# Group 0 of a Fourier-mixing network on one Trainium2 core: the mixture laid into y's tile before y arrives, and the second weight ahead of group 1

## The chip, the cores and the metric

The kernel runs on one core of a Trainium2 chip. The metric is the device time of one execution in microseconds, as the median of several runs; the runs and the profile of the kernel before are shown below. The engines of the core work side by side, each through its own list of instructions in order: TensorE (matmuls, PE in the trace), VectorE (DVE), ScalarE (ACT), GpSimd (POOL) and SyncE (SP), which here only issues DMAs.

## The reference

For x of 8 batches, 3136 tokens and 256 channels, a filter is applied in the frequency domain along the tokens; then a Fourier mixing over tokens and channels is added, the sum is normalised over its channels and goes through two weight matrices with a ReLU between them.

```python
X = np.fft.rfft(x, axis=1)
y = np.fft.irfft(X * (filt_r + 1j * filt_i)[None], n=3136, axis=1)
mixed = np.real(np.fft.fft(np.fft.fft(y, axis=1), axis=2))
u = y + mixed
un = (u - mean(u)) / sqrt(var(u) + 1e-6)          # over the 256 channels
out = u + np.maximum(un @ w_ch1, 0) @ w_ch2       # 256 -> 1024 -> 256
```

## The kernel before, in words

Fourier transforms are done as matmuls in stages. For batch b, `s1_b_*` and `s2_b_*` are the forward stages, `i1_b_*` and `y_b_*` the inverse ones. The spectrum, folded to half its length, lies in a ring `eo` of 1920 slots; a slot stands for a pair of tokens. Batch 0 is done in float32, ahead of everything; batches 1 to 7 in pairs of float16 numbers (a high half and the low rest). Between the stages data go through DRAM to be laid out anew: `d<-ast`, `at<-d`, `d<-bt`, `b<-d`, `dy<-ys`, `y<-dy`.

The second part of the network works on 49 groups of twice 128 slots. For a group g: `mix_g`, the mixture, is formed from the ring on TensorE (line 904); VectorE adds it to y, scaled, in eight instructions (line 914) and takes moments; ScalarE the root (968), VectorE the scales (974 to 978); `un`, `u` high and low halves (1058, 1061, GpSimd 1062); two DMA transposes give `ut` (1063); eight first products `h_g_f` of six matmuls 128 x 512 (1087), whose ReLU goes in halves through ScalarE (1097) and VectorE (1098); eight second products of twelve matmuls each into `acc_g` (1117); and y + beta acc goes out (1126). Group 0 is a special case (`prepare_first`): its y comes straight from the PSUM banks of the inverse stage, and its u is transposed on TensorE (`flip`, tiles `utt`).

The weights come as 64-bit words. They are widened to float32 (`widen`, four VectorE operations and one of ScalarE for each of eight parts), squared (`wsq`, ScalarE), bounded by a power of two (`bound_weights`, `pow2`, with one matmul `pb_w` that spreads a column) and split into halves (`split_weights`, `lower_weights`); parts 0 to 3 are the first weight, 4 to 7 the second. The tables LOAD_AT, WIDEN_AT, SQUARE_AT, BOUND_AT and SPLIT_AT say at which step each is put into the program (`weigh(n)`).

The program is written as generators (`advance` for the forward stages, `give` for the inverse ones, `prepare` for a group) and a loop over q = 8 g + f, in which the first product of (g, f) and the second product of the one LAG = 2 behind stand in turn. A scheduler orders the instructions of each engine; `after(...)` holds one behind a marked other. `warm(n)` puts n matmuls without use on TensorE (52 after the start, in the tile `idle`), so that it doesn't stand still.

Where instructions are named s2_1_0, i1_1_6 or y_1_0, this is the tile that they write: stage, batch, part.

## Time and profile before

| | us |
|---|---|
| runs | 1442.11, 1444.62, 1441.51 |
| median | 1442.11 |
| the profiled execution, its own time | 1443.13 |
| its span | 1441.4 |

In the profiled execution the engines were busy, in us of the span: TensorE 1399.5 (97%), VectorE 1045.9 (73%), ScalarE 758.2 (53%), GpSimd 508.3 (35%). The mean granted clock of TensorE was 0.996 of 2.4 GHz. The profile is read by its time lines (start of an instruction or of a run of equal ones, its length, and in brackets how long the engine stood idle before it and what ended that), by groups of instructions, and by stretches of time (length, then the busy time and the count of instructions of PE, PE's weight loads, DVE, ACT and POOL, the granted clock as a share of 2.4 GHz, the share of the DMA engines and GB/s). Matmuls are pipelined, so the length of a run of matmuls is longer than the time until the next can start.

### The profile page before, as it was taken

What the parts mean: (1) busy time and instruction counts of PE and PEld (TensorE: products, weight loads), DVE (VectorE), ACT (ScalarE), POOL (GpSimd) and SP (SyncE); (2) the same over time, 40 slices, a digit from 0 to 9 for tenths busy, and PEclk for the clock granted to TensorE, in tenths of its full rate; (3) what the DMA queues carried; (4) which work ended last, traced back from release to release, by engine and by line L of the source; (5) the groups of instructions that cost most, each with busy time, mean ns of one, the idle gap of its engine ahead of it and who ended that gap; (6) DMA issues with size and microseconds to landing.
All of it is one profiled execution on the core that took longest, in us unless ns stands there. A gap on an engine that the chain in (4) does not pass through costs nothing.

```text
span 1441.4 us, 30003 instructions
## 1 busy us (share of the span) xinstructions
PE 1399.5 (97%) x11274; PEld 946.7 (66%) x11274; DVE 1045.9 (73%) x2327; ACT 758.2 (53%) x1422; POOL 508.3 (35%) x641
## 2 busy tenths in 40 slices
...
GB/s 362 209 218 243 228 176 250 205 228 209 264 136 193 243 173 232 173 222 187 195 209 200 224 180 226 144 229 233 132 258 156 230 189 193 110 157 78 86 59 30
DMA packets 434221, 276.42 MB, mean 192 GB/s; under 512 B 218796, under 2 KB 401084, under 8 KB 434076
## 3 DMA queue, kind: packets, MB, share of 16 engines
...
q14 instruction: 57, 0.47, 0.1%
q10 hardware_dynamic: 128, 0.05, 0.0%
HBM read 124.41 MB, written 99.17 MB: 155 GB/s over the span
## 4 chain that ended last, share of the span: by engine, by line
PE 64%; DMA 10%; POOL 6%; issue 5%; DVE 4%; ACT 3%; SPq 2%; DVEq 0%; POOLq 0%; ACTq 0%
PE h L1087 25%; PE acc L1117 24%; PE s L495 3%; DMA at<-d 2%; PE y L814 2%; DMA x<-x 2%; PE mix L904 2%; DMA d<-ast 2%; POOL u L1062 1%; PE s L481 1%; PE i L694 1%; PE s L592 1%; PE i L696 1%; PE i L695 1%; POOL ef L639 1%
## 5 line engine op out<-in xcount | busy, mean ns | idle before, releaser
L1117 PE MATMUL acc<-w2s,h 128*128 128x256 f16 x4704 | 594.2, 273 | 2.0 <-DVE y L1126 1.4
L1087 PE MATMUL h<-ut,home 128*128 128x512 f16 x2352 | 580.2, 380 | 12.8 <-DVE h L1098 8.2
L1117 PEld LDWEIGHTS <-h 128*128 128x128 f16 x4704 | 455.8, 98 | 147.8 <-issue 18.2
L1097 ACT ACTIVATE h<-h 128x512 f16<-128x512 f32 x392 | 233.1, 595 | 383.3 <-PE h L1087 374.4
L1098 DVE SCALAR_TENSOR_TENSOR h<-h,h 128x512 f16<-128x512 f32 x392 | 267.5, 684 | 203.5 <-ACT h L1097 202.7
L1087 PEld LDWEIGHTS <-home 128*128 128x128 f16 x2352 | 221.5, 98 | 221.5 <-issue 31.7
L1062 POOL TENSOR_TENSOR u<-un,u 128x512 f16<-128x512 f32 x96 | 110.8, 1172 | 665.3 <-ACT u L1061 612.3
L914 DVE SCALAR_TENSOR_TENSOR y<-mix,alpha,y 128x508 f32<-128x508 f32 (+1 forms) x360 | 152.6, 475 | 1.7 <-DMA d<-bt 0.6
L1058 ACT ACTIVATE un<-y,sb 128x256 f32<-128x256 f32 x192 | 99.7, 590 | 33.4 <-DVE sb L978 29.6
L609 POOL TENSOR_TENSOR yt<-yt,t 128x224 f32<-128x224 f32 x108 | 73.3, 679 | 121.8 <-DVE t L601 48.8
L698 DVE TENSOR_TENSOR bt<-i,bt 112x512 f16<-112x512 f32 x98 | 66.6, 684 | 43.4 <-ACT bt L697 41.6
L825 ACT ACTIVATE ys<-y,alpha 128x512 f32<-128x512 f32 x98 | 66.5, 686 | 57.8 <-PE y L814 57.6
L1126 DVE SCALAR_TENSOR_TENSOR y<-acc,beta,y 128x512 f32<-128x512 f32 x98 | 71.1, 745 | 25.6 <-PE acc L1117 25.5
L697 ACT CAST bt<-i 112x512 f16<-112x512 f32 x98 | 56.8, 584 | 54.9 <-PE i L696 50.2
L639 POOL TENSOR_TENSOR ef<-yt 128x224 f32<-128x224 f32 x112 | 73.3, 674 | 33.2 <-ACT wsq_w L1148 15.7
L597 DVE SCALAR_TENSOR_TENSOR yt<-s,pF,ft 128x448 f32<-128x448 f32 x98 | 65.8, 674 | 26.3 <-PE s L593 19.3
L623 POOL TENSOR_TENSOR home<-yt,home 128x448 f16<-128x448 f32 x77 | 79.5, 1035 | 13.7 <-ACT home L622 13.6
L610 POOL TENSOR_TENSOR yt<-yt,t 128x224 f32<-128x224 f32 x108 | 74.7, 693 | 0.0
L962 DVE BATCH_NORM_STATS2 st<-y 128x6 f32<-128x256 f32 x196 | 72.8, 410 | 0.2
L306 DVE TENSOR_REDUCE mx<-x 112x1 f32<-112x1024 f32 x42 | 51.0, 1214 | 25.2 <-DMA x<-x 24.8
L601 DVE SCALAR_TENSOR_TENSOR t<-s,pF,ft 128x448 f32<-128x448 f32 x98 | 65.9, 674 | 0.0
L669 POOL TENSOR_TENSOR eo<-ef,eo 128x448 f16<-128x448 f32 (+6 forms) x55 | 51.6, 941 | 35.6 <-ACT eo L668 34.2
...
## 6 DMA issues: line engine op xcount, KB each, us to landing
...
```

What stands on the lines that cost most here:

```text
L609: nc.gpsimd.tensor_tensor(yh[:, 0], yh[:, 0], t2v[:, 1], op=ALU.subtract)
L610: marks["sum"] = nc.gpsimd.tensor_tensor(yh[:, 1], yh[:, 1], t2v[:, 0], op=ALU.add).ins
L623: nc.gpsimd.tensor_tensor(ylo, ytv, yhi, op=ALU.subtract)
L639: nc.gpsimd.tensor_tensor(ef[:, i], yt[:, 0, i], yt[:, 1, i], op=o)
L914: nc.vector.scalar_tensor_tensor(out, p, al, y, op0=ALU.mult, op1=ALU.add)
L962: nc.vector.bn_stats(st[:m, 2 * t + k], y[:m, t, k])
L1058: nc.scalar.activation(un[:m, k], y[:m, t, k], AF.Identity, bias=sb[:m, i, 1:2], scale=sb[:m, i, 3:4])
L1062: marks["u16", g] = nc.gpsimd.tensor_tensor(u16[:m, :, :, 1], unv, u16[:m, :, :, 0], op=ALU.subtract).ins
L1087: marks["pe"] = nc.tensor.matmul(p[:, c0 : c0 + n].rearrange("p (t k q) -> p t k q", k=2, q=m), homes["w1s"][:, d, hw, 128 * f : 128 * f + ...
L1097: marks["relu"] = nc.scalar.activation(h[:, 0, :nt], p[:, :nt], AF.Relu).ins
L1098: marks["h"] = nc.vector.scalar_tensor_tensor(h[:, 1, :nt], p[:, :nt], 0.0, h[:, 0, :nt], op0=ALU.max, op1=ALU.subtract).ins
L1117: nc.tensor.matmul(acc[:m, k], h[:, hh, c0 : c0 + m], w2s[:, f, hw], start=f == 0 and k == 0 and i == 0, stop=f == 7 and k == 1 and i == 2,)
```

## The change

For group 0 the mixture is copied out of PSUM already scaled (`near`, and `point` for the single row at half the sampling frequency), and laid into y's tile by two VectorE additions and a copy and, for the single row, by two GpSimd additions and a ScalarE copy. When y comes, one addition for each of the two tiles is left. Both tiles then have one root and one set of scales. The high halves of u are formed by ScalarE straight from y; `un`, in float32, goes to VectorE and is used for the low halves alone. Of the 52 matmuls without use behind the start 20 are left: 8 ahead of the mixture where there were 18, none behind it where there were 10, and 6 behind each of y_2 and y_3 where there were 4 behind each of y_2 to y_7. y_4 to y_7 stand behind the transposes of u.

In the head the parts of the second weight are widened, squared, bounded and split during the eight first products of group 0, which stand in one run on four PSUM banks; then all 96 second products of group 0, and group 1 (mixture, addition, `prepare`) behind the 28th of them. The filters' bound is taken later, and the first weight's earlier. Parts 4 and 5 of the weights are loaded to other buffers than before (LOAD_IN). The first forward stage of batch 1 comes later in the list of TensorE.

```diff
@@ constants
-LOAD_IN = ("b2", "b2", "ys", "ys", "b2", "b2", "ys", "ys")
-WIDEN_AT = (31, 33, 37, 41, 58.3, 58.3, 74, 74)
-SQUARE_AT = (44, 46, 58.1, 58.1, 68, 68, 1002, 1002)
-BOUND_AT = (58.2, 1003)
+LOAD_IN = ("b2", "b2", "ys", "ys", "ys", "ys", "b2", "b2")
+WIDEN_AT = (31, 33, 37, 41, 57.5, 1002, 1004, 1006)
+SQUARE_AT = (38, 42, 46, 47, 66, 1003, 1005, 1007)
+BOUND_AT = (56, 1008)
...
@@ turning u on TensorE (flip)
-            nc.tensor.transpose(pt[:q, i, :m], src[:, i], ident16[:m, :m])
+            with after("turn"):
+                marks["turn"] = nc.tensor.transpose(pt[:q, i, :m], src[:, i], ident16[:m, :m]).ins
...
@@ inverse step of batch 0
-                if j == 26:
-                    idle.append(ps_o.tile([128, 512], F32, tag="pso", name="idle"))
-                    warm(18, "i1", ("pb", "F"), p=idle[0])
...
-            with after("pe") if c == 0 and b else after("warm" if c < 8 else "pe") if b == 0 else nullcontext():
+            with after("pe") if c == 0 and b else after("warm" if c < 4 else "turn") if b == 0 else nullcontext():
...
-            if b == 0 and c < 8:
-                warm(4, "i2", p=idle[0])
-            with after("utt") if b == 0 else nullcontext():
+            if b == 0 and c < 4:
+                warm(6, "i2", p=idle[0])
+            with after("utt", ("cast", 0)) if b == 0 else nullcontext():
...
@@ group 0
-        nc.scalar.copy(near, pm)
-        marks["near"] = nc.scalar.copy(point[:1, 0], fix[0][2]).ins
-        pm, fix = near, [(t, row, point[:1, 0], a) for t, row, _, a in fix]
+        al = alphas[0]
+        nc.scalar.activation(near, pm, AF.Copy, scale=al[:, 0:1])
+        (t0, row, pn, _), = fix
+        marks["near"] = nc.scalar.activation(point[row, 0], pn, AF.Copy, scale=al[row, 0:1]).ins
+        y = mp.tile([128, 2, 2, 256], F32, tag="y", name="y_0", bufs=4)
+        yh = y.rearrange("p t k (h c) -> p t (k h) c", h=2)
+        even, odd = (
+            near[:, :, c0 : c0 + 127].unsqueeze(2).to_broadcast([128, 2, 2, 127]) for c0 in (1, 129)
+        )
+        nc.vector.tensor_tensor(yh[:, :, 0:4:3, 1:], even, odd, op=ALU.add)
+        nc.vector.tensor_tensor(yh[:, :, 1:3, 1:], even, odd, op=ALU.subtract)
+        nc.vector.tensor_copy(y[..., 0:129:128], near[:, :, 0:129:128].unsqueeze(2).to_broadcast([128, 2, 2, 2]))
+        for h, o in ((1, ALU.add), (0, ALU.subtract)):
+            with after("sum"):
+                marks["sum"] = nc.gpsimd.tensor_tensor(
+                    yh[row, t0, 2 + h, 1:], point[row, 0, 1:128], point[row, 0, 129:], op=o
+                ).ins
+        nc.scalar.copy(y[row, t0, 1, 0:129:128], point[row, 0, 0:129:128])
         yield
-        y = mp.tile([128, 2, 2, 256], F32, tag="y", name="y_0", bufs=4)
         ut = mp.tile([128, 2, 8, 128], F16, tag="ut", name="ut_0", bufs=2)
         mv, st, sb = small(0)
-        al = alphas[0]
         for t in range(2):
-            add(y[:, t], pm[:, t], al, sums[t])
-            for tf, row, pn, _ in fix:
-                if tf == t:
-                    add_nyquist(y[row, t, 1], pn, al[row], sums[t][row, 1])
+            nc.vector.tensor_tensor(y[:, t], sums[t], y[:, t], op=ALU.add)
             moments(0, y, [(t, groups[0][t])], st, mv)
-            roots(0, sb, mv, [(128, slice(2 * t, 2 * t + 2))])
-            yield
+        yield
+        parts = [(128, slice(0, 4))]
+        roots(0, sb, mv, parts)
+        scales(0, sb, mv, parts)
+        yield
         for t in range(2):
-            scales(0, sb, mv, [(128, slice(2 * t, 2 * t + 2))])
-            yield
             un = mp.tile([128, 2, 256], F32, tag="un", name=f"un_0_{t}", bufs=2)
             u16 = mp.tile([128, 2, 2, 2, 128], F16, tag="u16", name=f"u16_0_{t}", bufs=2)
-            unv = un.rearrange("p k (d q) -> p k d q", q=128)
             for k in range(2):
                 i = 2 * t + k
-                if t and k:
-                    nc.vector.tensor_scalar(un[:, k], y[:, t, k], sb[:, i, 3:4], sb[:, i, 1:2], op0=ALU.mult, op1=ALU.add)
-                else:
-                    nc.scalar.activation(un[:, k], y[:, t, k], AF.Identity, bias=sb[:, i, 1:2], scale=sb[:, i, 3:4])
-            marks["cast", 0] = nc.scalar.copy(u16[:, :, :, 0], unv).ins
+                marks["cast", 0] = nc.scalar.activation(
+                    u16[:, k, :, 0],
+                    y[:, t, k].rearrange("p (d q) -> p d q", q=128),
+                    AF.Identity,
+                    bias=sb[:, i, 1:2],
+                    scale=sb[:, i, 3:4],
+                ).ins
+                nc.vector.tensor_scalar(un[:, k], y[:, t, k], sb[:, i, 3:4], sb[:, i, 1:2], op0=ALU.mult, op1=ALU.add)
+            unv = un.rearrange("p k (d q) -> p k d q", q=128)
...
@@ first product
-        p = ps_h.tile([128, 512], F32, tag="psh", name=f"h_{g}_{f}")
+        pool, tag = (ps_o, "pso") if g == 0 and f % 4 > 1 else (ps_h, "psh")
+        p = pool.tile([128, 512], F32, tag=tag, name=f"h_{g}_{f}")
...
@@ the head of the main program
+    idle.append(ps_o.tile([128, 512], F32, tag="pso", name="idle"))
+    warm(8, "i1", ("pb", "F"), ("pb", "w1"), p=idle[0])
     for _ in mixture(0):
         pass
     first_group = prepare_first()
     next(first_group)
+    advance(59)
+    for ch in (2, 3, 6):
+        fold_of[0](ch)
     while come[0] < 1 + WAIT + 2:
-        weigh(63 + come[0])
-        if come[0] == 1:
-            warm(10, "mix", p=idle[0])
+        weigh(60 + come[0])
         give(come[0] + 1)
-    for i, _ in enumerate(first_group):
-        weigh(68 + i)
-        give(min(come[0] + 1, KEPT))
+    next(first_group)
+    give(come[0] + 2)
+    for _ in first_group:
+        pass
...
@@ the loop over groups
+            catch_up(8 if q == 8 else min(q - LAG, 2 * (q - 8) + 1))
         if g < ng:
             first_product(g, f)
-        if q == 0:
+        weigh(1002 + q)
+        if q == 7:
+            for part in range(4):
+                split_weights("w2", part)
             work = prepare(1)
-            for _ in range(AHEAD):
-                next(work, None)
-        if q == 1:
-            weigh(1002)
-        if q == 4:
-            weigh(1003)
-        if q in (4, 5):
-            split_weights("w2", 2 * q - 8)
-            split_weights("w2", 2 * q - 7)
-        for n, part, ch in ((2, 1, 4), (6, 0, 5), (6, 0, 6), (8, 1, 5), (9, 1, 6)):
+        for n, part, ch in ((3, 1, 2), (7, 0, 4), (8, 1, 3), (9, 0, 5), (9, 1, 4), (10, 1, 5), (11, 1, 6)):
             if q == n:
                 fold_of[part](ch)
         if q > 1:
             next(halves, None)
-        if f == 8 - AHEAD:
+        if f == 8 - AHEAD and g or q == 7:
             for _ in work:
                 pass
             if g + 2 < ng:
                 work = prepare(g + 2)
-        next(work, None)
+        if q > 7:
+            next(work, None)
         if q >= 8:
             catch_up(min(q - LAG + 1, 2 * (q - 8) + 2))
         give(min(come[0] + 1, soon(32 * q + SOON)))
-        advance(min(int(STEPS * (1 + min((q + 1) / RISE, (q + 1) / per + EARLY))), STEPS + 3 + 3 * (q - 3 if q > 3 else 0) if q < 16 else NB * STEPS))
-        for ahead in [2] * (q == 3) + [g + 3] * (f == 6):
+        advance(min(int(STEPS * (1 + min((q + 1) / RISE, (q + 1) / per + EARLY))), STEPS + 3 + 4 * (q - 6 if q > 6 else 0) if q < 14 else NB * STEPS))
+        for ahead in [2] * (q == 7) + [3] * (q == 11) + [g + 3] * (f == 6 and g > 0):
```

On VectorE, for group 0 (the tile y_925 is y of group 0, y_0_911 and y_1_918 are the PSUM banks of the inverse stage, st and mv the moments). Before:

```order
L914 SCALAR_TENSOR_TENSOR y_925<-near,alpha_652,y_0_911 128x4x127
L914 SCALAR_TENSOR_TENSOR y_925<-near,alpha_652,y_0_911 128x4
L914 SCALAR_TENSOR_TENSOR y_925<-near,alpha_652,y_925 128x2x127 x2
L914 SCALAR_TENSOR_TENSOR y_925<-near,alpha_652,y_1_918 128x4x127
L914 SCALAR_TENSOR_TENSOR y_925<-near,alpha_652,y_1_918 128x4
L914 SCALAR_TENSOR_TENSOR y_925<-point,alpha_652,y_0_911 1x2x127
L914 SCALAR_TENSOR_TENSOR y_925<-point,alpha_652,y_0_911 1x2
L962 BN_STATS st_928<-y_925 128x6
L914 SCALAR_TENSOR_TENSOR y_925<-near,alpha_652,y_925 128x2x127 x2
L914 SCALAR_TENSOR_TENSOR y_925<-point,alpha_652,y_925 1x127 x2
```

In the changed kernel (y_858 is y of group 0, y_0_907 and y_1_914 the banks; `size` belongs to a weight's widening):

```order
L997 TENSOR_TENSOR y_858<-near 128x2x2x127
L998 TENSOR_TENSOR y_858<-near 128x2x2x127
L999 COPY y_858<-near 128x8
L1156 SCALAR_TENSOR_TENSOR home<-size_882,home 128x512
L1010 TENSOR_TENSOR y_858<-y_0_907,y_858 128x512
L959 BN_STATS st_923<-y_858 128x6 x2
L960 BN_AGGR mv_922<-st_923 128x2 x2
L1010 TENSOR_TENSOR y_858<-y_1_914,y_858 128x512
L959 BN_STATS st_923<-y_858 128x6 x2
L960 BN_AGGR mv_922<-st_923 128x2 x2
L971 RECIPROCAL sb_924<-sb_924 128x4
```

Four scaled additions for each tile and four for the single row behind the banks have become two additions and a copy ahead of them and one addition for each tile behind.

On TensorE, from the first product of group 0 to that of group 1 (h_g_f a first product, acc_g_t the sums of the second ones of tile t, h16_g_f what they take, eo the ring, mix_g the mixture of group g, home the first weight, y_0_10 an inverse stage of batch 0). Before:

```order
L1087 MATMUL h_0_0_1100<-ut_0_926,home_596 128x512
L904 LDWEIGHTS eo_595
L904 MATMUL mix_1_1110<-mix_86,eo_595 128x129
...
L1087 MATMUL h_0_1_1171<-ut_0_926,home_596 128x512
...
L1117 LDWEIGHTS h16_0_6_1346
L1117 MATMUL acc_0_1_1429<-w2s_93,h16_0_6_1346 128x256
L1087 LDWEIGHTS home_596
L1087 MATMUL h_1_0_1442<-ut_1_1135,home_596 128x512
```

In the changed kernel:

```order
L1129 LDWEIGHTS h16_0_2_1073
L1129 MATMUL acc_0_0_1279<-w2s_93,h16_0_2_1073 128x256
L801 MATMUL y_0_10_1133<-b2_0_5_905,i2f_85 112x512
L801 MATMUL y_0_11_1149<-b2_0_5_905,i2f_85 112x512
L901 LDWEIGHTS eo_601
L901 MATMUL mix_1_1205<-mix_86,eo_601 128x129
...
L901 MATMUL mix_1_1205<-mix_86,eo_601 128x127
...
L1129 MATMUL acc_0_1_1280<-w2s_93,h16_0_7_1184 128x256
L901 LDWEIGHTS eo_601
L901 MATMUL mix_2_1394<-mix_86,eo_601 128x129
...
L1099 LDWEIGHTS home_602
L1099 MATMUL h_1_0_1381<-ut_1_1230,home_602 128x512
```

Mixture 1 has moved from behind the first of group 0's first products to a place behind the 28th of its second products, and all second products of group 0, not 84 of 96, stand ahead of h_1_0; mixture 2 begins right ahead of h_1_0.

On GpSimd, in batch 1's second step (yt a part of the filtered spectrum, ef and eo the folding into the ring, the rows with home and y_3 the low halves of z, the input of stage i1; u_4 the low halves of group 4). Before:

```order
L623 TENSOR_TENSOR home<-yt_5_2385,home 128x4x112
L623 TENSOR_TENSOR y_3_597<-yt_5_2385,y_3_597 128x4x112
L609 TENSOR_TENSOR yt_6_2524<-yt_6_2524,t_1_6_0_2543 128x224
L610 TENSOR_TENSOR yt_6_2524<-yt_6_2524,t_1_6_0_2543 128x224
L609 TENSOR_TENSOR yt_6_2524<-yt_6_2524,t_1_6_1_2598 128x224
L610 TENSOR_TENSOR yt_6_2524<-yt_6_2524,t_1_6_1_2598 128x224
L669 TENSOR_TENSOR eo<-ef_4_2518,eo 128x2x224
L1062 TENSOR_TENSOR u_4_0_2491<-un_0_2488,u_4_0_2491 128x4x128
L1062 TENSOR_TENSOR u_4_1_2564<-un_1_2561,u_4_1_2564 128x4x128
L623 TENSOR_TENSOR home<-yt_6_2524,home 128x4x112
```

In the changed kernel:

```order
L623 TENSOR_TENSOR home<-yt_5_2343,home 128x4x112
L652 TENSOR_TENSOR ef_4_2476<-yt_4_2198 1x224
L1073 TENSOR_TENSOR u_4_0_2449<-un_0_2446,u_4_0_2449 128x4x128
L623 TENSOR_TENSOR y_3_603<-yt_5_2343,y_3_603 128x4x112
L1073 TENSOR_TENSOR u_4_1_2522<-un_1_2519,u_4_1_2522 128x4x128
L609 TENSOR_TENSOR yt_6_2482<-yt_6_2482,t_1_6_0_2501 128x224
L669 TENSOR_TENSOR eo<-ef_4_2476,eo 128x2x224
L610 TENSOR_TENSOR yt_6_2482<-yt_6_2482,t_1_6_0_2501 128x224
L609 TENSOR_TENSOR yt_6_2482<-yt_6_2482,t_1_6_1_2556 128x224
L610 TENSOR_TENSOR yt_6_2482<-yt_6_2482,t_1_6_1_2556 128x224
L639 TENSOR_TENSOR ef_5_2611<-yt_5_2343 128x224 x2
L623 TENSOR_TENSOR home<-yt_6_2482,home 128x4x112 x2
```

The two operations of u_4 stood between the last part of yt and the low halves of z made from it; now they stand ahead of that part, with a low half of z of the part before between them.

## Rows read from the trace of the kernel before

**Rows 1.** The page's first part: busy us, share of the span and instructions of each engine.

```profile
PE 1399.5 (97%) x11274; PEld 946.7 (66%) x11274; DVE 1045.9 (73%) x2327; ACT 758.2 (53%) x1422; POOL 508.3 (35%) x641
```

**Rows 2.** Timeline of TensorE, 60 to 122: start, length, engine, line, operation, out<-in, count [idle before <-releaser].

```profile
60.46 4.05 PE L283 MATMUL idle<-still 128*128 128x512 bf16 x18
...
67.95 5.34 PE L776 MATMUL y<-b,direct 112*128 112x256 f32 x24
...
73.13 1.02 PE L804 MATMUL y<-b,i2f 112*112 112x512 f32 x2
...
73.99 1.03 PE L283 MATMUL idle<-still 128*128 128x512 bf16 x4
...
86.01 1.47 PE L1087 MATMUL h<-ut,home 128*128 128x512 f16 x6 [0.79 <-DVE ut L315]
...
97.84 1.46 PE L1087 MATMUL h<-ut,home 128*128 128x512 f16 x6 [1.74 <-DVE h L1098]
...
108.05 1.46 PE L1087 MATMUL h<-ut,home 128*128 128x512 f16 x6
...
109.34 6.39 PE L1117 MATMUL acc<-w2s,h 128*128 128x256 f16 x57
...
115.63 1.46 PE L1087 MATMUL h<-ut,home 128*128 128x512 f16 x6
...
118.80 1.46 PE L1087 MATMUL h<-ut,home 128*128 128x512 f16 x6 [1.72 <-DVE h L1098]
...
121.33 3.69 PE L481 MATMUL s<-x,s1f 112*112 112x512 f32 x8 [1.02 <-DMA s1f<-c_s1f]
```

**Rows 3.** VectorE's groups, 71 to 77: line, operation, names, shapes, count, busy us, mean ns, idle before.

```profile
L914 DVE SCALAR_TENSOR_TENSOR y<-near,alpha,y 128x254 f32<-128x254 f32 (+2 forms) x8 | 4.1, 571 | 0.0
```

**Rows 4.** Timeline of VectorE, 95 to 103, group 1.

```profile
95.49 1.64 DVE L914 SCALAR_TENSOR_TENSOR y<-mix,alpha,y 128x254 f32<-128x254 f32 x4
...
97.72 0.74 DVE L962 BATCH_NORM_STATS2 st<-y 128x6 f32<-128x256 f32 x2
...
102.47 0.17 DVE L976 SCALAR_TENSOR_TENSOR sb<-mv,sb 128x4 f32<-128x4 f32 x1
```

**Rows 5.** Timeline of ScalarE, 105 to 111.

```profile
105.31 2.06 ACT L1058 ACTIVATE un<-y,sb 128x256 f32<-128x256 f32 x4
...
108.23 1.13 ACT L1061 CAST u<-un 128x512 f16<-128x512 f32 x2
...
109.83 1.05 ACT L457 ACTIVATE xsq<-x 112x1024 bf16<-112x1024 f32 x1
```

**Rows 6.** Timelines of GpSimd and of SyncE's queue, 108 to 114, group 1.

```profile
108.92 2.28 POOL L1062 TENSOR_TENSOR u<-un,u 128x512 f16<-128x512 f32 x2 [15.75 <-ACT u L1061]
...
110.93 2.72 SPq L1063 DMA_TRANSPOSE ut<-u  x2
```

**Rows 7.** Timeline of TensorE, 291 and 361, batch 2's second and inverse steps.

```profile
291.25 0.23 PE L592 MATMUL s<-s,at 112*128 112x56 f16 x1 [2.40 <-DMA at<-d]
...
361.12 0.32 PE L694 MATMUL i<-z,i 112*112 112x256 f16 x1 [1.55 <-DMA z<-home]
```

**Rows 8.** Stretches of 1 us, 291 and 294: busy us (count), clock, DMA share, GB/s.

```profile
291.00:292.00 1.00, 0.74 (x16) 0.75 (x17) 0.00 (x0) 0.17 (x1) 0.00 (x0) 0.50 1.09 320
...
294.00:295.00 1.00, 1.00 (x14) 0.60 (x11) 1.00 (x4) 0.00 (x0) 1.00 (x2) 0.80 0.47 164
```

**Rows 9.** Timeline of TensorE, 155 to 232, batch 1: s2_1_0, i1_1_6 and y_1_0.

```profile
155.36 0.19 PE L592 MATMUL s<-s,at 112*128 112x56 f16 x1
...
215.99 0.32 PE L694 MATMUL i<-z,i 112*112 112x256 f16 x1
...
231.25 1.06 PE L814 MATMUL y<-b,i 112*64 112x256 f16 x12 [1.12 <-DMA b<-d]
```

**Rows 10.** Stretch from 180 to 200, columns as in group 8.

```profile
180.00:200.00 20.00, 19.28 (x221) 15.01 (x219) 19.90 (x42) 9.39 (x19) 19.79 (x28) 1.00 0.86 184
```

**Rows 11.** Timeline of SyncE's queue, 212: the last transpose of z of batch 1.

```profile
212.13 1.30 SPq L627 DMA_TRANSPOSE z<-home  x1
```

38 lines of the change are left out of this document (16 added, 22 removed).

## The prediction

> **What bounds the kernel now.** I read the page's busy times first: TensorE is busy 1399.5 us, 97% of the span [rows 1], so a change is worth only the idle time of TensorE that it removes or makes, plus the useless matmuls that it drops. Then the timeline of TensorE over the head of the program, where the change lies [rows 2], the groups and timelines of the engines that TensorE waits for there [rows 3 to 6], and the stretches further on whose order the change shifts [rows 7 to 11]. The reader is to see that the head is a chain through every engine (mixture, add, moments, root, u, transposes, first product), filled up with dummies, and that behind it batch 1's second step hangs on GpSimd.
>
> Useful matmuls are the same in both kernels. By the two orders TensorE runs the same sequence again from about group 13 on, so the whole difference is made in about the first 450 us, and I follow it in five terms, each against the profiled execution of 1443.13 us (span 1441.4). That execution lies 1.02 us above the median of the three runs, 1442.11; I add the terms to it and take 1.0 off at the end.
>
> **Term 1, up to the first product of group 0: 3.5 us earlier.** Dummies fall from 52 to 20; eighteen took 4.05 us, 0.22 each from start to start [rows 2]. Ten go ahead of the mixture; that frees about 1 us only, because eo's low halves from VectorE must be there first. The ten behind the mixture go, and y_0's 24 matmuls (5.34 us) start about 1.5 us earlier, at 66.4, and end at 71.8. On VectorE eight scaled adds of 4.1 us [rows 3] and four for the single Nyquist row lay mostly behind y_0's first matmuls. Now the mixture is laid into y's tile by two operations of some 508 elements and a small copy, beside y_0's matmuls, and what is left behind them is one 512-element add per tile (0.6 us each, an estimate from the 508-element form). Behind the second add: 1.1 us of moments and 1.3 of root and scales [rows 4], 0.7 for a copy of y_3 that stands ahead on ScalarE, about 1.9 for the four casts of u's high halves (four un took 2.06 [rows 5]) and 0.8 for the last low half: 78.2. The last transposes end at 79.1, and y_4 to y_7, now behind the transposes, take 0.86 each (73.13 to 73.99 [rows 2]) and fill the 3.4 us in which ut is copied: h_0_0 at 82.5 instead of 86.01 [rows 2]. Bounds: 1.5 earlier (only the dummies behind the mixture count) to 7.0 (all 32 dummies that go, at 0.22).
>
> **Term 2, up to the second product of group 0.** Eight first products of 1.29 us (108.05 to 109.34 [rows 2]) in one run, on four PSUM banks instead of two, and y_8, y_9 end at 94.7. The run loses the waits that stood in it, the longest 1.74 us. But the second weight's scale comes behind the last square: reduction, root, lines, the broadcast matmul, two exponent steps, then a high and a low half, some 2.9 us; the low half ends about 97.2, so TensorE waits about 2.5 us in front of acc_0. The place gains against before, since nothing of group 1 stands in front, but what follows needs group 1.
>
> **Term 3, up to batch 1's second step: 1.4 us later than before.** Mixture 1 now stands behind the 28th matmul of acc_0 and y_10, y_11 (see the order): 97.2 + 28 x 0.11 + 2 x 0.86 + 0.9 (16 matmuls with a quarter of a first product's columns) = 102.9. TensorE's remaining filling is 68 matmuls at 0.11 (57 in 6.29 us [rows 2]) and ten of mixture 2: empty at 110.9. Group 1's path from the end of its mixture is 8 adds at 0.41 and four moments at 0.37 with two aggregates (5.2), 1.3 for the root and five dependent scales of 0.17 with the gaps between them [rows 4], 2.06 for four un, 0.56 for the first cast [rows 5], 2.0 from GpSimd's first operation to the first transpose and 2.72 for both [rows 6], and 1.5 to land (before, both were issued at 113.65 and h_1_0 had them at 115.63, so at most 2.0 [rows 2, 6]): 15.3, so h_1_0 at about 118.3, a wait of 7.4 us. Before, mixture 1 lay between the first products and h_1_0 came at 115.63 without a wait [rows 2]. After has then done 12 second-product matmuls more (1.3 us) and 6 of mixture less (0.3): 1.7 behind. Next, before loses 1.72 and 1.02 us (h_1_1, table s1f [rows 2]); the table now comes early, but ScalarE's squares of x (1.05 each [rows 5]), three of them between the reliefs of h_1_0 and h_1_1, cost about 1.4: 1.3 regained. The clock: the granted clock was 0.50, that is 1.2 GHz, in the stretch after the 2.40 us wait at 291.25 [rows 7, 8], while after the 1.74 us wait at 97.84 six matmuls took the usual 1.46 [rows 2]. A wait of 7.4 us is longer than either, and the fall at 291 (0.50 in three of the four slices from 291 to 295, 0.80 in the last [rows 8], 0.26 us of them idle) cost about 1.6 us of matmul time; I take 1.1, since part lies in the wait for h_1_1. Sum: 1.7 - 1.3 + 1.1, about 1.4. Bounds: -7.0 (no wait at h_1_0, no fall) to +4.5 (two falls, one at the 2.5 us wait too).
>
> The Trainium skill, "TensorE: Matmul & The Clock Gate", section "HAM oscillation — how this bites in real kernels", says that a TensorE that pauses for its data between batches of matmuls drops to the slow clock at each pause, and advises to run the work without pauses. It speaks against this change, which puts one long pause in the place of several short ones; the trace agrees at 291 and shows no fall at 97.84. By it alone the head would cost the full 1.6 for each of the two waits, 3.2 instead of 1.1.
>
> **Term 4, batch 1's second step: 3.6 us later.** From s2_1_0 (155.36) to y_1_0 (231.25) before takes 75.9 us [rows 9] with 72.1 of matmuls. By the order 48 second and 24 first-product matmuls, 10.5 us, have gone ahead of that stretch, so TensorE has only 61.6 to do in it. What remains is GpSimd's: 19.79 busy of 20 us between 180 and 200 [rows 10]; the transpose that its last low halves of z feed was issued at 212.13 [rows 11], so that i1_1_6 at 215.99 [rows 9] had its data barely in time. Its idle time could give back about 3 us. So i1_1_6 cannot come before about 57 us after s2_1_0, and with 12 more for bt, its way through DRAM and the load of b, y_1_0 not before 69: 7.4 lost against 3.8 before. GpSimd has u_4 in two pieces ahead of the last yt in the new order, which does not shorten it. Bounds: 0 (the first 12 us of filling that went ahead were slack) to 6.6 (y_1_0 follows i1_1_6 by 15.26 as before [rows 9]).
>
> **Term 5, batch 2: 1.3 us earlier.** Between s1_2_13 and s2_2_0 the order has 6 first and 9 second-product matmuls more, 2.3 us, which fill the 2.40 us wait at 291.25; with it the fall of the clock goes. But the next wait, 1.55 us at 361.12 [rows 7], hangs on the same chain (z), so most of it comes back there; by the order TensorE stands 1.1 us better at i1_2_6. Bounds: 0 to -4.0 (2.4 + 1.6, nothing late next).
>
> Shifts that cost nothing by my reading: the filters' bound taken later, the first weight's squares earlier, and widenings spread over h_0 (VectorE and ScalarE idle there; without that cover three operations of 512 elements, 0.56 each by the casts of rows 5), the zeros moved to the start, SP's order of loads. b_0_5, now behind the seventh weight's buffer, lands about 1 us before its use.
>
> **Sum.** Terms 1 and 2 are contained in term 3, whose place in time is worked out from theirs. 1443.13 + 1.4 + 3.6 - 1.3 = 1446.8; less 1.0: 1445.8.
>
> **The rivals.**
> (B) Faster: group 1's transposed tile is there when acc_0 ends, so the 7.4 us wait and the fall are gone: -5.7 - 1.3 in term 3, + 3.6 - 1.3, about -4.7: 1437.4. For it: every engine on that path has little else then. Against it: the sum of 15.3 us from durations alone. It decides when the path is shorter than 8.0 us; at half of the wait the sum is 1442 to 1443, no change.
> (C) No change: GpSimd's stretch has slack or moves along with TensorE, term 4 is 0: 1443.13 + 1.4 - 1.3 - 1.0 = 1442.2; or term 5 is the full -4.0, 1443.1. For it: before waits only 1.12 us at y_1_0 [rows 9]. Against it: GpSimd's 19.79 of 20 [rows 10].
> (D) Slower still: the 2.5 us wait before acc_0 drops the clock as 2.40 did at 291, mixture 1 and with it h_1_0 come 1.6 to 3 later: 1448 to 1449.
> (E) The change does not do what it says, since the scheduler reorders it: the orders of VectorE and TensorE exclude that.
>
> **Chances.** Forecast 0.36 with its own range 1445 to 1447.5; B 0.24; C 0.30; D 0.10. Faster by over 0.2% (2.9 us, about what a measurement of this kernel tells from no change) needs B, or C with part of B: 0.27. Within 0.2%: 0.31, slower: 0.42. The range reaches from B to beyond D: 1437.0 to 1451.5.
>
> **What would show it.** Right: h_0_0 near 82.5, a wait of 5 to 8 us on TensorE at h_1_0 near 118 with the clock at 0.5 behind it, s2_1_0 near 168 to 169, waits on z or b of together 6 to 8 us until y_1_0, no wait at s2_2_0. Wrong: h_1_0 before 114, or y_1_0 less than 65 us behind s2_1_0.

## The result, and the profile after

The changed kernel takes 1458.79 us (median of four executions, 1457.53 to 1461.95), the kernel before 1441.81 beside it (four, 1440.08 to 1444.62): ratio 1.012 with the interval 1.0103 to 1.0137. It is slower, as the likeliest case said, but by 16.7 us in the profiled executions (1459.86 against 1443.13) and not by 3.7, and the time lies outside the range. The page's first line of the changed kernel (columns as in [rows 1]):

```profile
PE 1399.5 (96%) x11242; PEld 948.1 (65%) x11242; DVE 1042.5 (71%) x2317; ACT 757.2 (52%) x1421; POOL 509.0 (35%) x643
```

TensorE is busy for the same 1399.5 us as in [rows 1], although it issues 32 dummies less (7.0 us at 0.22): about as much came back as matmuls at half the clock, which count as busy for twice as long. The span less the busy time went from 41.9 us to 58.6. The mean granted clock fell from 0.996 to 0.990.

The timeline of TensorE in the head of the changed kernel, 67 to 130 (columns as in [rows 2]):

```profile
67.96 8.20 PE L773 MATMUL y<-b,direct 112*128 112x256 f32 x24 [2.11 <-DMA b<-d_f]
...
86.43 10.53 PE L1099 MATMUL h<-ut,home 128*128 128x512 f16 x48
97.58 1.94 PE L801 MATMUL y<-b,i2f 112*112 112x512 f32 x4 [0.63 <-ACT h L1109]
...
101.32 0.38 PE L1129 MATMUL acc<-w2s,h 128*128 128x256 f16 x2 [1.32 <-ACT w2s L1225]
102.11 3.00 PE L1129 MATMUL acc<-w2s,h 128*128 128x256 f16 x26 [0.41 <-DVE w2s L1212]
105.55 1.97 PE L801 MATMUL y<-b,i2f 112*112 112x512 f32 x4 [0.44 <-DMA b<-d_f]
107.36 0.96 PE L901 MATMUL mix<-mix,eo 128*128 128x129 f16 x16
108.15 7.59 PE L1129 MATMUL acc<-w2s,h 128*128 128x256 f16 x68
...
121.59 0.40 PE L901 MATMUL mix<-mix,eo 128*128 128x129 f16 x2 [5.46 <-ACT eo L672]
123.83 4.90 PE L1099 MATMUL h<-ut,home 128*128 128x512 f16 x12 [1.83 <-DMA ut<-u]
```

Read it against [rows 2]. y_0 starts where it did, at 67.96 (67.95 before), since it waits for its data b; TensorE now stands still for 2.11 us in front of it, and the 24 matmuls take 8.20 us instead of 5.34. The run of h_0 is whole (48 matmuls in 10.53). Mixture 1 ends at 108.15, and group 1's first product starts 15.7 us behind that. TensorE has 68 second products and eight matmuls of mixture 2 for this time, and stands still for 5.46 and 1.83 us. Stretches of 1 us (columns as in [rows 8]) show what came of both waits:

```profile
67.00:68.00 1.00, 0.04 (x1) 0.07 (x1) 1.00 (x4) 0.15 (x1) 0.00 (x0) 0.50 1.09 384
68.00:69.00 1.00, 1.00 (x3) 0.82 (x4) 1.00 (x3) 0.00 (x0) 0.53 (x1) 0.50 0.85 270
...
74.00:75.00 1.00, 1.00 (x7) 0.87 (x6) 0.97 (x4) 0.00 (x0) 1.00 (x2) 1.00 1.03 415
...
123.00:124.00 1.00, 0.17 (x1) 0.10 (x2) 0.45 (x1) 0.70 (x2) 1.00 (x2) 0.50 1.15 245
...
127.00:128.00 1.00, 1.00 (x3) 0.30 (x2) 0.69 (x1) 1.00 (x2) 0.00 (x0) 0.50 1.08 378
```

The clock is the third number from the right: 0.50, that is 1.2 GHz, at and behind both waits. With it three or four matmuls of y_0 stand in a us (PE's count is the first in brackets), at 1.00 seven.

Then batch 1's second step, TensorE at 175, 221 and 248, to be read against [rows 9]:

```profile
175.46 0.20 PE L592 MATMUL s<-s,at 112*128 112x56 f16 x1 [1.31 <-DMA at<-d]
...
177.01 0.20 PE L592 MATMUL s<-s,at 112*128 112x56 f16 x1 [0.55 <-DMA at<-d]
...
220.65 0.96 PE L901 MATMUL mix<-mix,eo 128*128 128x129 f16 x16 [1.26 <-DVE t L601]
225.80 0.43 PE L691 MATMUL i<-z,i 112*112 112x256 f16 x1 [4.18 <-DVE st L959]
...
248.18 1.06 PE L811 MATMUL y<-b,i 112*64 112x256 f16 x12 [2.26 <-DMA b<-d]
```

From s2_1_0 (175.46) to y_1_0 (248.18) it is 72.7 us, against 75.9 before; in this time TensorE has only 61.3 us of useful matmuls in place of 71.7 (each counted by its time at full clock), so 11.5 us are lost in place of 4.2. The wait of 4.18 us is put down to VectorE; by GpSimd's and SyncE's timelines it is the transpose of the sixth part's low halves of z:

```profile
219.84 1.16 POOL L1073 TENSOR_TENSOR u<-un,u 128x512 f16<-128x512 f32 x1 [0.56 <-ACT u L1072]
220.96 1.03 POOL L623 TENSOR_TENSOR y<-yt,y 128x448 f16<-128x448 f32 x1
221.96 1.14 POOL L1073 TENSOR_TENSOR u<-un,u 128x512 f16<-128x512 f32 x1
```

SyncE's queue at the same place:

```profile
221.16 1.29 SPq L1074 DMA_TRANSPOSE ut<-u  x1
222.54 1.26 SPq L627 DMA_TRANSPOSE z<-y  x1
```

GpSimd does u_4's first half (L1073) ahead of that low half (L623, 220.96); the transpose follows at 222.54, and the stage that reads it starts at 225.80. The order of GpSimd quoted with the change has these three rows in this order. The last low halves of z, GpSimd's end of the chain, before and after:

```profile
209.67 1.04 POOL L623 TENSOR_TENSOR home<-yt,home 128x448 f16<-128x448 f32 x1
...
227.75 2.03 POOL L623 TENSOR_TENSOR home<-yt,home 128x448 f16<-128x448 f32 x2
```

They end 55.3 us behind s2_1_0 before and 54.3 after.

Where the two executions part is seen when TensorE's starts are compared at equal useful work. At h_1_0 the new kernel is 8.2 us later but has done 1.0 us more work: 7.2 behind. In the same way it is 8.1 behind at s2_1_0 (20.1 later, 12.0 more work), 15.3 at y_1_0 (16.9 later, 1.6 more), and 16.7 at the end. Predicted were 1.7, 1.4, 5.0 and 3.7. So nearly all is lost by 248 us, in two places: the head, and batch 1's second step. Behind it gains and losses alternate. Apart from one at the very end in both, the clock falls are at 291, 810 and 957 us before, 3.4 us each, and at 67, 121, 224 (6.8 us each), 326 and 487 (3.4 each) now.

### The profile page after: what moved, and what is told of

Same layout as the page of the kernel before. It is cut to its first block, busy times and chain, and to the rows that moved or that the text cites. A ratio compares the mean times of both kernels' runs of the same rounds, so it can differ in the third digit from the quotient of the medians.

```text
span 1458.1 us, 29943 instructions
## 1 busy us (share of the span) xinstructions
PE 1399.5 (96%) x11242; PEld 948.1 (65%) x11242; DVE 1042.5 (71%) x2317; ACT 757.2 (52%) x1421; POOL 509.0 (35%) x643
## 4 chain that ended last, share of the span: by engine, by line
PE 70%; DMA 9%; DVE 5%; issue 5%; POOL 4%; ACT 2%; SPq 2%; DVEq 0%; ACTq 0%; POOLq 0%
PE h L1099 27%; PE acc L1129 26%; PE s L496 3%; PE y L811 3%; DMA x<-x 2%; PE mix L901 2%; DMA at<-d 2%; DMA d<-ast 2%; PE i L691 1%; PE s L482 1%; PE s L592 1%; PE i L692 1%; PE i L693 1%; DVE y L911 1%; PE s L593 1%
## 5 line engine op out<-in xcount | busy, mean ns | idle before, releaser
L1099 PE MATMUL h<-ut,home 128*128 128x512 f16 x2352 | 581.7, 381 | 10.7 <-DVE h L1110 8.2
L1073 POOL TENSOR_TENSOR u<-un,u 128x512 f16<-128x512 f32 x96 | 111.3, 1176 | 678.6 <-ACT u L1072 606.1
L1138 DVE SCALAR_TENSOR_TENSOR y<-acc,beta,y 128x512 f32<-128x512 f32 x98 | 71.2, 745 | 23.1 <-PE acc L1129 22.9
L623 POOL TENSOR_TENSOR home<-yt,home 128x448 f16<-128x448 f32 x77 | 79.4, 1035 | 13.8 <-ACT home L622 13.8
L901 PEld LDWEIGHTS <-eo 128*128 128x128 f16 x784 | 48.5, 99 | 29.1 <-ACT eo L672 6.0
L901 PE MATMUL mix<-mix,eo 128*128 128x129 f16 (+2 forms) x784 | 60.1, 216 | 7.7 <-ACT eo L672 5.5
```

Of the source, the lines that this page charges most:

```text
L623: nc.gpsimd.tensor_tensor(ylo, ytv, yhi, op=ALU.subtract)
L901: marks["mix"] = nc.tensor.matmul(p[:, c0 : c0 + n], lhs(int(i > 2), hs), mix[:, hm, w0 : w0 + n], start=start and i == 0, stop=stop and i ...
L1073: marks["u16", g] = nc.gpsimd.tensor_tensor(u16[:m, :, :, 1], unv, u16[:m, :, :, 0], op=ALU.subtract).ins
L1099: marks["pe"] = nc.tensor.matmul(p[:, c0 : c0 + n].rearrange("p (t k q) -> p t k q", k=2, q=m), homes["w1s"][:, d, hw, 128 * f : 128 * f + ...
```

## The experiments

All ratios are against the kernel before on the same chip, with their 95% intervals; the medians of before were 1442.3 (e1, e3, e5, e7), 1442.88 (e4, e10, e11, e13), 1445.21 (e15 to e18) and 1442.93 (e19 to e21). "After" is the changed kernel. A loss at equal work is found as above, in the profiled execution of each.

**e5: before, with the new mixture of group 0 alone** (the whole part "group 0" of the diff, nothing else).

> The kernel before with group 0's new preparation alone (mixture laid into y's tile, one root, u's high halves straight from y); dummies, weights and all else as before. Theory A: h_0_0 comes 1.5 to 2 us earlier than 86.0 (a shorter path behind y_0), and 0 to 2 us of it reach the end: 1440 to 1442. Theory B (this part is itself a cost: ScalarE and VectorE forms that are longer, a GpSimd step on the path): h_0_0 not earlier than 86, end 1442 to 1445.

1440.42 us, 0.9982 (0.9963 to 1.0001), not told apart from before. TensorE's timeline in e5:

```profile
68.03 5.34 PE L776 MATMUL y<-b,direct 112*128 112x256 f32 x24
...
82.05 1.47 PE L1101 MATMUL h<-ut,home 128*128 128x512 f16 x6 [0.79 <-DVE ut L315]
```

With the ten dummies kept in front, y_0 runs at the full clock and h_0_0 comes at 82.05. This part does what it says: the path from y_0's end to h_0_0 is 4 us shorter, even with y_4 to y_7 and their dummies still ahead of the transposes.

**e7: before, without the ten dummies behind the mixture.**

```diff
-                    with after("warm"):
+                    with after("mix"):
...
-        if come[0] == 1:
-            warm(10, "mix", p=idle[0])
```
(the first line keeps y_0 behind the mixture, now that there are no dummies to keep it behind)

> The kernel before without the ten dummies behind mixture 0 and nothing else changed. Theory A (the clock): TensorE waits 2 us or more for b in front of y_0, the granted clock falls to 0.50 over y_0, whose 24 matmuls take near 8.2 us instead of 5.34, and the end is 2 to 3 us later, near 1444.5. Theory B (dummies only delay y_0): y_0 starts 1 to 2 us earlier, no fall, end 0 to 1.5 us earlier.

1444.55 us, 1.0019 (1.0002 to 1.0037), 2.2 us slower, just clear of noise. TensorE waits 1.79 us in front of y_0, which then starts at 68.44 and takes 5.42 us, without a fall. The clock fell later, for 3.4 us from 88.3, in h_0_0, behind three more waits (1.06, 0.29 and 0.79 us). The size is that of the first theory, the place of the fall isn't.

**e1: after, with these ten dummies.**

```diff
-                    with after("mix"):
+                    with after("warm"):
...
+        if come[0] == 1:
+            warm(10, "mix", p=idle[0])
```

> The changed kernel with ten dummies put back behind mixture 0, ahead of y_0. Theory A (the clock): the dummies cover the wait for b, the granted clock stays at 1.00 from 66 to 74, y_0's 24 matmuls take 5.3 us instead of 8.20, h_0_0 comes near 83.5 instead of 86.43, and the end moves by about -2.9 us, to 1456. Theory B (the head is only as long as the weights' and group 1's path): h_0_0 comes earlier, but the wait at h_1_0 grows by as much, and the end stays within 1 us of 1458.8.

1459.31 us, 1.0117 (1.0089 to 1.0145): no change from after. TensorE's timeline in e1:

```profile
68.45 5.42 PE L773 MATMUL y<-b,direct 112*128 112x256 f32 x24
...
84.14 10.53 PE L1099 MATMUL h<-ut,home 128*128 128x512 f16 x48
96.89 2.91 PE L801 MATMUL y<-b,i2f 112*112 112x512 f32 x4 [2.23 <-DMA b<-d_f]
...
101.24 0.59 PE L1129 MATMUL acc<-w2s,h 128*128 128x256 f16 x2 [1.33 <-ACT w2s L1225]
```

The 2.3 us that y_0 gives back are lost again in front of y_8, which waits 2.23 us, and acc_0 starts where it did (101.24, 101.32). SyncE's queue in e1 shows why:

```profile
89.73 0.43 SPq L747 DMA_DIRECT2D b<-d_f  x1
90.26 3.15 SPq L452 DMA_DIRECT2D x<-x  x4
```

And ScalarE in e1:

```profile
98.14 0.58 ACT L824 COPY ys<-y 112x512 f32<-112x512 f32 x1 [2.23 <-PE y L801]
98.62 0.21 ACT L1201 ACTIVATE mw<-mw 128x1 f32<-128x1 f32 x1
```

b for y_8 (512 KB) is issued at 89.73, when the seventh part of the weights has been widened out of its buffer, and lands 7 us later, with four loads of x (512 KB each) right behind it (how much of the 7 us is theirs, e20 below shows). The root of the second weight's bound (L1201) stands behind the copy of y_8 in ScalarE's list, and with it everything up to acc_0. This is a second wait beside the first; in after, where y_0 is late, y_8 waits only 0.63 us, and that for ScalarE.

**e19 and e20: those loads of x behind b, in after and in e1.**

```diff
-            with after(("y", 1), ("un", 0)) if b == 1 and q > 2 else after(("b", 1)) if b == 1 else nullcontext():
+            with after(("y", 1), ("un", 0), ("b", 5)) if b == 1 and q > 2 else after(("b", 1)) if b == 1 else nullcontext():
```

> The changed kernel with the loads 3 to 6 of batch 1's x issued behind that of b_0_5 (by the order mixture 1 then stands ahead of acc_0 too). Theory A (b_0_4's slow landing sets y_8 and through the copy of y_8 the second weight's root): no wait on b at y_8; since h_0_7 ends at 97 here, acc_0 gains only 0.5 to 1 us, but group 1's path starts 3 to 5 us earlier with mixture 1 in front, and h_1_0 comes at 118 to 121: end 1454 to 1457. Theory B (the widening on VectorE sets acc_0, and group 1 in front delays it): acc_0 later than 101.3, end 1458 or more.

> The same with the ten dummies behind mixture 0. Theory A (the wait and fall at y_0 cost 2.3 us, which the late b_0_4 hid): h_0_0 near 84.1, acc_0 2 to 2.5 us earlier than in the run without the dummies, and the end as much: 2 to 4 us less than that run. Theory B (the y_0 wait is hidden by another chain as well): the same end within 1 us.

e19 takes 1462.76 us, 1.0137 (1.0104 to 1.0169), e20 1459.6, 1.0118 (1.0076 to 1.0159). With the loads in this order the dummies are worth their 3 us as far as h_1_0: h_0_0 comes at 83.72 in e20 against 86.55 in e19, h_1_0 at 121.68 against 124.90. At equal work 2.5 us are left of it at s2_1_0 and 1.6 at y_1_0. The medians differ by 3.2, but the intervals overlap. In both acc_0 is later than in after (105.38 and 102.30 against 101.32; mixture 1 now stands ahead of it), so the loads' order is no cure by itself. Nor are the loads of x the main part of b's 7 us: in e20, where they stand behind, b for y_8 is issued at 89.29 and used at 95.45, 6.2 us later and behind a wait of 1.20. Group 1 still waits; TensorE's timeline in e20:

```profile
118.20 0.40 PE L901 MATMUL mix<-mix,eo 128*128 128x129 f16 x2 [4.69 <-ACT eo L672]
...
121.68 3.57 PE L1099 MATMUL h<-ut,home 128*128 128x512 f16 x8 [2.05 <-DMA ut<-u]
```

y_0's wait and about half of y_8's are mended here, and 6.7 us of waits at mixture 2 and h_1_0 are left, nearly as in after (5.46 + 1.83).

**e4: after, with group 1 begun at the first of group 0's first products, as before.**

```diff
+        if q == 0:
+            fold_of[1](2)
+            fold_of[1](3)
             work = prepare(1)
+            for _ in range(AHEAD):
+                next(work, None)
...
```
(and group 1's additions no longer wait for the second weight's low halves; the two folds go from their later places)

> The changed kernel with group 1 prepared at the first of group 0's first products, as in the kernel before (its mixture there, its adds no longer held behind the second weight's low halves), and the folds that its mixture reads moved ahead of it. Theory A (the wait of some 7 us at h_1_0 with its clock fall is the head's largest loss): h_1_0 no longer waits for its transposes by more than 2 us, no fall there, the place where it and the 96 second products are done comes 5 to 7 us earlier than in the changed kernel; batch 1's second step still loses its time (its chain has no more filling than before): end 1451 to 1454. Theory B (in-order queues: group 1's work on VectorE delays the second weight's widening and scale, so acc_0 comes as much later): the head's gain is under 2 us, end 1456 to 1460.

1464.54 us, 1.0157 (1.013 to 1.0183). TensorE's timeline in e4:

```profile
107.05 3.73 PE L801 MATMUL y<-b,i2f 112*112 112x512 f32 x4 [9.19 <-DMA b<-d_f]
...
113.39 0.38 PE L1099 MATMUL h<-ut,home 128*128 128x512 f16 x1
```

The wait at h_1_0 is gone, as foreseen, and y_8 waits 9.19 us in its place. b for y_8 can be loaded only when the seventh part of the weights has been read out of its buffer, and here the last to read it is ScalarE (`size`, L1154). ScalarE and SyncE's queue in e4:

```profile
101.18 1.09 ACT L1069 ACTIVATE un<-y,sb 128x256 f32<-128x256 f32 x2 [1.06 <-DMA x<-x]
102.18 0.64 ACT L1154 ACTIVATE size<-raw 128x512 f32<-128x512 f32 x1
...
102.85 0.36 SPq L747 DMA_DIRECT2D b<-d_f  x1
```

`size` stands in ScalarE's list behind group 1's root (99.83) and `un`, which wait for the additions and moments of group 1 on VectorE. VectorE's own three reads of that buffer are done by 91.2. The new place of group 1 and the new buffers of the weights depend on each other.

**e13, e15, e16 and e17: together with other parts.** e13 is e4 with the ten dummies and batch 1's first step begun as early as before (the line of e3 below). e15 is after with the buffers of parts 4 and 5 of before:

```diff
-LOAD_IN = ("b2", "b2", "ys", "ys", "ys", "ys", "b2", "b2")
-WIDEN_AT = (31, 33, 37, 41, 57.5, 1002, 1004, 1006)
+LOAD_IN = ("b2", "b2", "ys", "ys", "b2", "b2", "ys", "ys")
+WIDEN_AT = (31, 33, 37, 41, 57.5, 57.8, 1004, 1006)
```

e16 is e13 with the same two lines, e17 is e1 with them and the early first step.

> The changed kernel with the ten dummies behind mixture 0, group 1 prepared at the first product of group 0 and batch 1's forward stages at the rate of before, all three; what is left of the change is group 0's new preparation and the tables of the weights' loads and widenings. Theory A (the three together are the loss): end 1440 to 1445. Theory B (the weights' tables, with the loads of b behind the widenings and the second weight's root behind a copy that waits for y_8, cost by themselves): h_0_0 earlier than 84, but a wait of 2 to 5 us on b or on the second weight in front of acc_0, end 1446 to 1450.

> The changed kernel with weight parts 4 to 7 loaded to the buffers of before (4 and 5 to those of b, 6 and 7 to those of ys) and part 5 widened ahead of y_0, so that the loads of b_0_4 and b_0_5 no longer stand behind widenings 6 and 7. Theory A (these loads, and the second weight's root behind a copy that waits for y_8, set acc_0): acc_0 1 to 3 us earlier than 101.32, no wait on b at y_8 to y_11; of it 1 to 3 us reach the end, since batch 1's second step still lacks its filling: 1455 to 1458. Theory B (the widening that now stands in front of y_0 costs as much): 1458 to 1461.

> The kernel with the ten dummies, group 1 at group 0's first products and batch 1's stages early (which came out at 1466 us with a wait of 8.6 us at y_8), and besides the loads of b freed as in the kernel above. Theory A (the 8.6 us wait is b_0_4's load, held by widening 6, and what followed it came from there): that wait goes, and the end is 1440 to 1448. Theory B (the wait is VectorE's and ScalarE's queues, with group 1, the widenings and the reliefs of h in one place): a wait of 5 us or more stays there, end above 1455.

> The changed kernel with the ten dummies, batch 1's forward stages at the early rate and the loads of b freed; group 1 stays late, behind the 96 second products. Theory A (batch 1's first stage fills the wait for group 1 and batch 1's second step keeps its filling): h_1_0's wait falls under 3 us, 4 to 6 us lost between s2_1_0 and y_1_0, end 1444 to 1450. Theory B (group 1's lateness costs its 7 us and a clock fall wherever batch 1 stands): end 1451 to 1456.

e13: 1466.07, 1.0166 (1.014 to 1.0191); y_8 waits 8.60. e15: 1472.59, 1.0192 (1.0158 to 1.0226); the widening that now comes early delays u (the transposes wait 4.86 for ScalarE), and h_0_0 comes at 93.27. e16: 1474.06, 1.0202 (1.0173 to 1.023); 15.01 us of waiting for the second weight's lines. e17: 1457.62, 1.0097 (1.0067 to 1.0126): in batch 1's second step it loses only 2.2 us, but at equal work it is 15.9 us behind before at h_1_0 and 14.7 at s2_1_0 (4.26 and 3.31 us of it are waits for the second weight). In none did the pieces of before and after add up; each moved the wait to another place on VectorE's or ScalarE's list.

**e3: after, with batch 1's first step begun as early as before.**

```diff
-        advance(min(int(STEPS * (1 + min((q + 1) / RISE, (q + 1) / per + EARLY))), STEPS + 3 + 4 * (q - 6 if q > 6 else 0) if q < 14 else NB * STEPS))
+        advance(min(int(STEPS * (1 + min((q + 1) / RISE, (q + 1) / per + EARLY))), STEPS + 3 + 3 * (q - 3 if q > 3 else 0) if q < 16 else NB * STEPS))
```

> The changed kernel with batch 1's forward stages written as early as in the kernel before (3 steps for each q above 3). Theory A (batch 1's second step is a chain of some 73 us whatever stands beside it, and the 10 us of filling that went ahead of s2_1_0 are what is missing): s2_1_0 stands about as much work into the program as before, y_1_0 follows with 4 to 5 us lost instead of 11, and the end is 5 to 8 us earlier, 1451 to 1454. Theory B (the loss behind 130 us comes from u_4 standing ahead of the last halves of z on GpSimd, and from clock falls): no gain from the earlier stage, within 2 us of 1458.8.

1455.56 us, 1.0094 (1.0064 to 1.0124), some 3 us less than after (the two intervals just overlap). s2_1_0 starts at 160.13, with 72.1 us of matmuls from there to y_1_0; the step takes 77.5 us and loses 5.4. TensorE in front of y_10 and of h_1_0, in e3:

```profile
103.66 3.54 PE L801 MATMUL y<-b,i2f 112*112 112x512 f32 x4 [4.55 <-DMA b<-d_f]
...
127.71 0.56 PE L901 MATMUL mix<-mix,eo 128*128 128x129 f16 x8
128.11 1.92 PE L482 MATMUL s<-x,s1f 112*112 112x512 f32 x4
129.87 2.75 PE L1099 MATMUL h<-ut,home 128*128 128x512 f16 x12
```

h_1_0 starts later than in after, since matmuls of batch 1's first step (L482) now stand in front of it, but it has no wait. The head is hardly better for it: e3 waits 4.55 us for b in front of y_10 instead, and at h_1_0 it is 6.8 us behind before at equal work, where after is 7.2. The gain is in the second step. At equal work e3 is 6.6 us behind before at y_1_0, where after is 15.3 behind: the one line gives back 8.7 us there. Of these the end keeps some 6 in the profiled executions (1453.74 against 1459.86).

**e21: e20 with the same line.**

> The changed kernel with x behind b_0_5, the ten dummies, and batch 1's forward stages at the rate of before. Theory A (head and missing filling together are the loss): 4 to 6 us lost between s2_1_0 and y_1_0, end 1444 to 1451. Theory B (group 1 late costs its path wherever it stands, some 7 us with a clock fall): a wait of 5 us or more at h_1_0 or for s1_1's data, end 1452 to 1457.

1452.66 us, 1.007 (1.0047 to 1.0094), the fastest of those that keep group 1 late; its executions lie far apart (1446.13 to 1459.46, the profiled one is the lowest), which I can't explain. 5.9 us are lost in the step, as the first theory has it. The head is no better here either: at h_1_0 e21 is 9.1 us behind before at equal work.

**e10: after, with u_4 behind z's halves** (ScalarE's `un` of group 4 behind `zh`, GpSimd's u_4 behind `zl`).

```diff
+                with after("zh") if g == 4 else nullcontext():
...
+            with after("zl") if g == 4 else nullcontext():
```

> The changed kernel with group 4's un on ScalarE and u_4 on GpSimd held behind the low halves of z that are ready at that place. Theory A (the wait of 4.18 us in front of i1_1_5 comes from u_4 and un standing ahead of z_5's second half): that wait falls to 0 to 2.5 us, with it the clock fall at 224, and 2 to 5 us reach y_1_0 and the end: 1454 to 1457. Theory B (the chain of batch 1's second step is as long without them): another wait of the same size takes its place by y_1_0, end within 1.5 us of 1458.8.

1468.7 us, 1.0177 (1.0149 to 1.0205). TensorE's timeline in e10:

```profile
220.78 0.37 PE L691 MATMUL i<-z,i 112*112 112x256 f16 x1 [2.87 <-DVE bt L695]
...
229.70 0.43 PE L691 MATMUL i<-z,i 112*112 112x256 f16 x1 [3.85 <-DMA z<-y]
```

The wait at the same stage is 3.85 (4.18), one of 2.87 stands ahead of it, and group 4's first product now waits 6.41 for ut; the clock stays at half for 23.9 us. Neither theory foresaw that. Moving u_4 does not take the wait away; e10 does not show what causes it, since it holds ScalarE's `un` as well and so makes group 4 late.

**e11: e5 with the table s1f loaded earlier**, at the stage's first step and into another buffer.

```diff
+                if k == 0 and b in PLAIN:
+                    table = fp.tile([112, 112], F32, tag="t2", name=f"s1f_{b}", bufs=2)
+                    nc.sync.dma_start(table, a["c_s1f"])
...
```
(the load in front of the stage goes, and group 0's part is as in e5)

> The kernel before with group 0's new preparation and with batch 1's table s1f loaded among the loads of x instead of in front of its first stage. Theory A: the wait of 1.39 us for the table in front of s1_1_0 goes, nothing else is late there, and the end is 1 to 1.5 us earlier than with the preparation alone: 1438 to 1440. Theory B (the table's wait covers the next one, the squares of x and their bound, or the shifted order makes a new wait in batch 1 or 2): same as with the preparation alone or later, 1440 to 1443.

1436.68 us, 0.9956 (0.9939 to 0.9974): faster than both kernels (from e5 its interval doesn't part it). Its profiled execution is the slowest of its twelve (1445.17). The table's wait of 1.02 us [rows 2] is gone (the first matmuls on x follow at 119.25 without a wait).

**e18: e11 with group 1 late, no other part of the change** (its start moved from q == 0 to q == 7, all second products of group 0 ahead of it).

```diff
-            catch_up(min(q - LAG, 2 * (q - 8) + 1))
+            catch_up(8 if q == 8 else min(q - LAG, 2 * (q - 8) + 1))
...
-        if q == 0:
+        if q == 7:
             work = prepare(1)
-            for _ in range(AHEAD):
-                next(work, None)
...
-        if f == 8 - AHEAD:
+        if f == 8 - AHEAD and g or q == 7:
...
-        next(work, None)
+        if q > 7:
+            next(work, None)
```

> The kernel before with group 0's new preparation and the early table (1436.7 us), and of the rest of the change only that all 96 second products of group 0 stand ahead of group 1, which is prepared at the eighth first product; weights' tables, dummies and batch 1's rate as before. By the order batch 1's first stage then stands ahead of mixture 1. Theory A (group 1 late costs little where other matmuls fill the wait, since batch 1's stages stand early): 1437 to 1441. Theory B (group 1 late costs its wait and a clock fall, 5 to 8 us): 1442 to 1446.

1458.81 us, 1.0103 (1.0076 to 1.0129), where e11 has 0.9956: 0.0147 of 1443, some 21 us between the medians, by this alone. TensorE's timeline in e18:

```profile
117.52 0.96 PE L904 MATMUL mix<-mix,eo 128*128 128x129 f16 x16
...
139.38 4.91 PE L1101 MATMUL h<-ut,home 128*128 128x512 f16 x12 [11.79 <-DMA ut<-u]
```

And a stretch of 1 us in e18:

```profile
130.00:131.00 1.00, 0.00 (x0) 0.00 (x0) 0.72 (x5) 0.11 (x1) 0.00 (x0) 0.55 1.13 233
```

From the end of mixture 1 (118.3) to h_1_0 it is 21.1 us here, 5.4 more than in after: VectorE has `ast` of batch 1's first step and two outputs of group 0 to do between group 1's operations. In e18:

```profile
123.90 0.74 DVE L1140 SCALAR_TENSOR_TENSOR y<-acc,beta,y 128x512 f32<-128x512 f32 x1
124.55 1.00 DVE L914 SCALAR_TENSOR_TENSOR y<-mix,alpha,y 128x254 f32<-128x254 f32 x3
125.46 0.75 DVE L484 SCALAR_TENSOR_TENSOR ast<-s,sx,ast 112x512 f16<-112x512 f32 x1
```

And e18 is an overdose: 84 of group 0's 96 second products stand ahead of mixture 1, where after has 28. TensorE runs dry, waits 11.79 us, and has the clock at half for 13.7 us from 130.1. At equal work e18 is 16.1 us behind e11 at h_1_0 and 13.1 at the end of the profiled executions. Some 4.4 of the 16.1 are lost ahead of acc_0 already, with a wait of 4.97 us for VectorE between group 0's first products, which e11 doesn't have. So it shows that a late group 1 alone can cost as much as the whole change loses, and how; after is 7.2 behind at h_1_0, and how much of this is group 1's lateness by itself no run shows. The other parts tried by themselves moved the time by -1.9 (e5) and +2.2 us (e7).

The starts and lengths of these executions side by side, in us (W: useful matmul time from s2_1_0 to y_1_0; lost: the difference):

| | h_0_0 | acc_0 | h_1_0 | s2_1_0 | s2_1_0 to y_1_0 | W | lost |
|---|---|---|---|---|---|---|---|
| before | 86.0 | 105.1 | 115.6 | 155.4 | 75.9 | 71.7 | 4.2 |
| after | 86.4 | 101.3 | 123.8 | 175.5 | 72.7 | 61.3 | 11.5 |
| e1 | 84.1 | 101.2 | 124.6 | 176.3 | 74.6 | 64.0 | 10.7 |
| e3 | 86.0 | 110.6 | 129.9 | 160.1 | 77.5 | 72.1 | 5.4 |
| e5 | 82.1 | 101.8 | 113.3 | 153.1 | 75.0 | 71.7 | 3.3 |
| e17 | 89.5 | 111.4 | 138.1 | 172.9 | 72.1 | 69.8 | 2.2 |
| e18 | 85.1 | 105.2 | 139.4 | 169.7 | 75.7 | 71.3 | 4.4 |
| e21 | 83.7 | 103.7 | 131.3 | 163.6 | 77.1 | 71.2 | 5.9 |

In all 17 kernels the step takes 72.1 to 80.8 us, with some 58 to 72 us of matmuls beside it. The nine with 58 to 66 us of matmuls lose 7.4 to 21.1 us in it (e10 the most, e16 the least); of the eight with 70 to 72 us seven lose 2.2 to 5.9. The eighth is e11, whose profiled execution loses 8.4 beside 72 us, so missing matmuls are not the only thing that can make the step lose time.

Of the ranges written down before the runs, the time lay outside both theories' in eight of the 15: above both in e4, e10, e13, e15, e17 and e18, below both in e11, between them in e3. Most of these put parts of the change together in a new way, and another wait came up.

## Why the prediction was right in direction and wrong in size

In the profiled executions 16.7 us were lost and 3.7 forecast. Of the 13.0 between, 6.7 belong to terms 1 to 3 (8.1 behind at s2_1_0 against 1.4), 3.6 to term 4 (7.2 against 3.6) and 2.7 to term 5 (1.4 later against 1.3 earlier). The upper bounds of the terms add up to 1453.2, above the stated 1451.5 and still below the 1458.79 measured. Of the signs named beforehand the wait at h_1_0 (7.3 us, clock 0.50 behind it) and those on z and b (4.18 and 2.26 us) came; h_0_0 near 82.5, s2_1_0 at 168 to 169 and s2_2_0 without a wait did not.

**Term 1 failed in its first step.** Right was the length from y_0's end to h_0_0: 10.7 us predicted, 10.3 measured in after and in e1 (8.7 in e5, where y_4 to y_7 stand elsewhere; that h_0_0 comes at 82.05 there, near the 82.5 predicted, is luck, since y_0 starts 1.6 us later than predicted). Wrong was "y_0's 24 matmuls (5.34 us) start about 1.5 us earlier, at 66.4". They start at 67.96: y_0 waits for b, which [rows 2] could not show, since the dummies filled TensorE up to the moment when b came. I had them down as what holds y_0 up, and did not ask when b lands. SyncE's queue answers that: the first of the four loads of b is issued at 64.20 in after and at 64.72 in e7, and y_0, waiting in both, starts 3.8 and 3.7 us behind it. In the kernel before it is issued at 63.93, so b was there at about 67.7, an estimate from these two, and the dummies held y_0 up by some 0.3 us and not 1.5. Without them the wait of 2.11 us drops the clock, 2.9 us on y_0's matmuls: h_0_0 at 86.43 and not 82.5. The clause on the clock's fall, weighed for h_1_0 and the wait before acc_0, was not applied to the place where the cover was taken away.

**Term 2 had the right length and missed a wait.** From h_0_0 to acc_0 14.7 us were predicted, 14.9 came. But of the loads behind the weights' buffers only "b_0_5, now behind the seventh weight's buffer, lands about 1 us before its use" was looked at, and costed at nothing (its use at y_10 waits 0.44 us for it in after and 4.55 in e3). b_0_4, for y_8 and y_9, is a wait as long as the one in front of y_0 (e1), coupled through a buffer to VectorE's widening and through ScalarE's list to the second weight's root. In after it stays hidden, since y_0 is late.

**Term 3 had the path right and its start wrong.** Group 1's path was 15.3 us predicted, 15.7 measured; the wait 7.4 predicted, 5.46 + 1.83 = 7.3 measured, the first part in front of mixture 2's second half. The start, the end of mixture 1, came at 108.15 instead of 102.9, and with it h_1_0 at 123.83 instead of 118.3: 7.2 behind and not 1.7. Behind it, two more sizes: the fall behind h_1_0 costs 2.15 us on the first twelve first products alone (4.90 us; 2.75 for the same run at the full clock in e3) instead of 1.1, and at s2_1_0 1.31 + 0.55 us of waiting for `at` were not foreseen. Of the 8.1 us at s2_1_0, e20 against e19 shows that y_0's wait and fall are worth 2.5 once x stands behind b. The wait in front of h_1_0 goes when batch 1's first step stands there (e3, e21), but others come in its place, and at equal work h_1_0 gains 0.4 us at most by it. The head is several waits that cover each other; no run takes all of them away.

**Term 4 named the mechanism, at half its size.** Predicted were 7.4 us lost against 3.8, measured 11.5 against 4.2: 7.3 us more and not 3.6. The filling that went ahead was as counted (61.6 us left by the count, 61.3 measured); the chain was not 69 us but 72.7. "Its idle time could give back about 3 us" was the step that failed: GpSimd gave back 1.0 (its last low half of z ends 54.3 us behind s2_1_0, 55.3 before), i1_1_6 came 59.2 us behind s2_1_0 (60.6 before), and from there to y_1_0 it is 13.5 us and not 12, for which no row stood. A second thing was put at nothing: the wait of 4.18 us drops the clock, and the 24 matmuls behind it (225.80 to 232.07) take 2.4 us more than at full speed, as a part of the 11.5; i1_1_6 then follows without a wait. (The term's upper bound of 6.6 is 6.9 by its own figures, 57 + 15.26 - 61.6 - 3.8.) That u_4 ahead of z's low half "does not shorten it" was true, but it is no cause by itself (e10). e3 shows the term by itself: with 72 us of matmuls in the step after's loss of 11.5 us goes to 5.4; e17 and e21, with other changes as well, lose 2.2 and 5.9.

**Term 5 had the sign of its first half.** The wait of 2.40 us at s2_2_0 [rows 7] fell to 1.41, and no fall follows. TensorE in batch 2's and batch 3's inverse steps:

```profile
308.79 0.20 PE L592 MATMUL s<-s,at 112*128 112x56 f16 x1 [1.41 <-DMA at<-d]
...
324.69 0.29 PE L691 MATMUL i<-z,i 112*112 112x256 f16 x1 [1.82 <-DMA z<-home]
...
486.11 0.32 PE L691 MATMUL i<-z,i 112*112 112x256 f16 x1 [2.65 <-DMA z<-home]
```

But two waits for z drop the clock instead, at 326 and 487 (3.4 us each), and a fall of before at 810 is missing: from y_1_0 to the end 1.4 us more are lost, where 1.3 less was forecast. Which of these follow from the change and which from its lateness no run separates, and 3 us there need no cause in the change: e7, the same kernel as before from y_1_0 on, is 2.5 us behind before at y_1_0 and 0.6 ahead at the end.

**The rivals.** B needed a path under 8 us; it is 15.7. C needed slack in GpSimd's stretch; the runs with less filling there lose more, as counted below the table, with e11 as the exception. D named a fall at the wait before acc_0; that wait is 1.32 us here, and no fall follows. The fall that came first is in front of y_0, where no rival stood. The Trainium skill, "TensorE: Matmul & The Clock Gate", section "HAM oscillation — how this bites in real kernels", advises to keep the work free of waits for data. The trace agrees at two of three places in the head: the clock is at 0.50 behind the waits at y_0 and at h_1_0, which costs 2.9 and at least 2.15 us, and does not fall at acc_0. The prediction's 3.2 us by that section was for h_1_0 and acc_0; that there were two falls, as it had counted, is in part luck.

**The version to keep** is e11, the mixture of group 0 and the earlier table without anything else: the part of the change that shortens a chain, without the part that moves filling away from two others.
